# A fused forward and backward pass: loading a third weight slab ahead of the rows, fixed places for the turns, and a PSUM half for the convolution

## The chip, the cores and the metric

The kernel runs on one core of a Trainium2 chip. A core has TensorE (PE), which multiplies matrices and also transposes; VectorE (DVE); ScalarE (ACT); GpSimd (POOL) and SyncE (SP). Every engine works off its own list of instructions in order. SP, ACT and POOL also issue DMAs, and such an issue stands in the engine's order like any other instruction. The metric is the device time of one execution in microseconds (us), as the median of several runs.

## What is computed

Cut to what matters, with S = 2048 rows, D = 1024 columns and F = 3584 hidden columns in bf16:

```python
x  = A_q
xn = layernorm(x)                                   # per row
# A: gated long convolution
k_shift = sum over 4 taps of shifted k * A_shift_k  # along the rows
kv = k_shift * v
y  = irfft(rfft(kv) * rfft(A_ssm_k))[:S] + kv * A_ssm_D   # per column
s  = xn * y
# B: bilinear unit
g, u = xn @ w_gate, xn @ w_up
bm = (g * u) @ w_down
out = x + s * silu(bm)
# returned: out and the gradients of all ten inputs for a given grad_out
```

## The kernel before

Rows are handled in blocks of 128 (16 blocks), columns of D in 8 groups of 128 (`dc`), and the hidden columns F in 14 slabs of 256 (`SLW`); a slab is 256 columns of both `w_up` and `w_gate` (1 MB). The kernel first forms g and u for all blocks and slabs ("units"), with the forward convolution laid between the units; then the down product, the output, and the backward pass, which is by far the larger part of the time.

**The start stage.** Row blocks come in six chunks, `chunks = [(0,1), (1,1), (2,2), (4,4), (8,4), (12,4)]` (first block, number of blocks). For each chunk `ln_load` (line 555) issues the load of the rows on SP, and `layer_norm` (line 566) does the statistics on DVE (`bn_stats`, lines 572 to 577), a square root on ACT (`half_r`, line 580), the rest of the factor and the normalisation on DVE (line 591), and a store of the normalised rows to DRAM (`XNd`) on POOL. The normalised rows are turned by PE (transposes into the PSUM tile `tr`; lines 597, 608 and 617) and copied by ACT into the transposed rows `XNT` (tiles U0 to U3; lines 598, 609 and 618). The turns of chunks 8 and 12 are not made at once: `turn_late` makes them after the first block of the next unit.

**A unit.** `gu_unit(sl, b0, n, w, tick)` multiplies n blocks from b0 by slab sl. For each block, 8 matmuls (line 656, one for each `dc`, 128x512) fill one of two PSUM buffers `psg`; ACT casts the buffer into `gut` (line 658). After the unit's last block, ACT issues the store of `gut` to `GUd` (`sta`, line 72). During the next unit, DVE multiplies the two halves (`hN`, line 213), POOL stores that to `Hd` (line 66), and some blocks later PE transposes `hN` (line 689), ACT copies it (`hT`, lines 691 and 693) and SP stores it to `HTd`.

**The order of loads.** SP issues the loads of chunks 0 and 1, slab 0, chunk 2, slab 1, and then chunks 4, 8 and 12. A slab is two DMAs of 512 KB:

```python
for a, wsrc in ((0, B_w_up), (1, B_w_gate)):
    last = eng.dma_start(out=w[:, :, a, :], in_=wsrc[:, fs].rearrange("(dc p) f -> p dc f", p=P))
```

The units of the start stage are, by chunk:

```python
([(0, 0)], [(1, 0), (0, 1), (1, 1)], [(2, 0), (2, 1)], [(3, 0), (3, 1)], [(4, 0)], [(5, 0)])[i]
```

where the first number is the chunk's place in `chunks` and the second the slab. After the start stage come slab 1 for chunks 8 and 12, and then slabs 2 to 13 for all blocks. Every DMA signals its end on one of a few semaphores that are used in turn; a DMA whose turn falls on a semaphore still in use waits on its issuing engine for the earlier one to end.

**The convolution.** `conv_forward` is a generator of small pieces: loads of k and v on POOL, the four shifted products of k on DVE (`shift`), and the transforms, which are matmuls against a table `TF` on PE (PSUM tiles `psF` and, for the inverse, `psY`) with products on DVE between them. The table is made by ACT from angles that DVE masks (line 174). A `tick` after each block of a unit pumps as many pieces as the share of work done so far asks for, so the pieces' places among the units are fixed when the program is built. The down product (`bm_first`, `late_mm`; matmul at line 994) then goes on pumping, and the inverse pieces of the convolution stand at steps `at = (52, 55, 58, 61)` of it.

Of the kernel before, what the change touches and what calls it, by code (L numbers as in the profile page):

```python
# [19 lines left out]
def build_kernel(  # L20
# [11 lines left out]
    nc = tc.nc  # L32
# [254 lines left out]

    def fwd8_half(x, i, SP, psp, first=None, held=False):

        pe_us[0] += 0.87  # L290
        for j in range(2):
# [4 lines left out]
            nc.scalar.copy(out=SP[:, :, j], in_=ps[:].rearrange("p s k x -> p s (k x)"))  # L296

    def fwd8(SPs, X, W, C, ahead, late=False):
# [225 lines left out]
    ps_tr = pool("ps_tr", 1, space=PSUM)  # L524
    ps_gu = pool("ps_gu", 2, space=PSUM)
    ps_st = pool("ps_st", 4, space=PSUM)
# [19 lines left out]

    def load_slab(sl, eng):
        w = fw.tile([P, DC, 2, SLW], BF16, name="wslab")
# [12 lines left out]

    tr_ln, act_copy = [None], [None]
    turn_rows = []

    def layer_norm(b0, n, x4):
# [22 lines left out]
        for i in range(n):  # L588
            b = b0 + i
            q, qi = divmod(b, 4)  # L590
            last = V.tensor_scalar(x4[:, i, :], x4[:, i, :], mv[:, i, 0:1], RSTD[:, b:b + 1], op0=SUB, op1=MUL)
            if b < 2:
                for hh in range(2):
                    ps = ps_st.tile([P, 4, P], BF16, name="tr")
                    for dc in range(4):
                        d0 = (4 * hh + dc) * P
                        tr_ln[0] = nc.tensor.transpose(ps[:, dc, :], x4[:, i, d0:d0 + P], ident[:])
                    act_copy[0] = nc.scalar.copy(out=XNT[0][:, 4 * hh:4 * hh + 4, b * P:b * P + P], in_=ps[:])
                if b == 0:
                    with tc.issue_after(tr_ln[0].ins):  # L600
                        keep_busy(10)
                continue
            if b0 >= 8:
                turn_rows.append((x4[:, i, :], q, qi))
                continue
            ps = ps_st.tile([P, DC, P], BF16, name="tr")
            for dc in range(DC):
                tr_ln[0] = nc.tensor.transpose(ps[:, dc, :], x4[:, i, dc * P:(dc + 1) * P], ident[:])
            act_copy[0] = nc.scalar.copy(out=XNT[q][:, :, qi * P:(qi + 1) * P], in_=ps[:])
# [30 lines left out]
    def gu_unit(sl, b0, n, w, tick):  # L640

        if n == 4:
            turn_of[0] += 1
            if turn_of[0] % 3 == 0 and sl < NSL - 2:
                gut = U[5][:, 2048:4096].rearrange("p (a i f) -> p a i f", a=2, i=4)
            else:
                gut = fg.tile([P, 2, 4, SLW], BF16, name="gut")
            hN = fg.tile([P, 2, 4, P], BF16, name="hN", bufs=3)
        else:
            gut = lnp.tile([P, 2, 2, SLW], BF16, name="gut_s", bufs=6)  # L650
            hN = lnp.tile([P, 2, 2, P], BF16, name="hN_s", bufs=6)
        for i in range(n):
            q, qi = divmod(b0 + i, 4)
            ps = ps_gu.tile([P, 512], F32, name="psg")
            for dc in range(DC):
                gu_mm[0] = nc.tensor.matmul(ps[:], XNT[q][:, dc, qi * P:(qi + 1) * P],  # L656
                                            w[:, dc].rearrange("p a f -> p (a f)"), start=(dc == 0), stop=(dc == DC - 1))
            nc.scalar.copy(out=gut[:, :, i], in_=ps[:].rearrange("p (a f) -> p a f", a=2))  # L658
# [42 lines left out]

    conv_state = {"forward": True, "filters": True}

    y_first = [None]

    def conv_forward():
# [83 lines left out]
        def half(ds, x, i, first=None):  # L790
            if (ds, int(first is not None)) not in EIGHT:
                return fwd4_half(x, i, cf, ps_cv, first)
            SP = cf.tile([P, 2, 2, 512], F32, name="SP", bufs=2)
            fwd8_half(x, i, SP, ps_cv, first, True)
            return SP

        def transform(ds, kind, sp, X, C, ahead, step):

            if ds == 7 and kind == 1:
                S_["forward"] = False  # L800
            if (ds, kind) in EIGHT:
                W = fwd4_buf(cs)[:].rearrange("p a b c x -> p (a b c) x")
                for n, w in enumerate(fwd8(sp, X, W, C, ahead, True)):
                    if n in (0, 2, 4, 6):
                        step()
                    yield net(w)
                return
# [24 lines left out]
        for ds in range(8):  # L832
# [16 lines left out]
            next(tl, None)  # L849
            room = cf.tile([P, 4, 256], F32, name="room", tag="hx")[:] if eight else None  # L850
            yield from transform(ds, int(ds > 0), sph, HX if ds else KX, room, nop1 if eight else lambda c: h_rows(ds + 1, c),
# [7 lines left out]
            if eight:  # L859
                h_rows(ds + 1, 1)  # L860
            if ds == 7:
                cf.release()
                S_["filters"] = False
            st(HFd[ds], HX[:])
# [14 lines left out]
        for _ in tl:  # L879
# [9 lines left out]
    chunks = [(0, 1), (1, 1), (2, 2), (4, 4), (8, 4), (12, 4)]  # L889
    xs = [(b0, n, u8((4, 6, 7)[b0 // 4 - 1], a=4) if n == 4 else lnp.tile([P, n, D], BF16, name=f"x{b0}")[:])  # L890
          for (b0, n) in chunks]
    for c in xs[0:2]:
# [3 lines left out]
    slabs.append(load_slab(1, nc.sync)[0])  # L896
    for c in xs[3:]:
        ln_load(*c)

# [38 lines left out]
    ps_st.release()  # L938
    ps_cv = pool("ps_cv", 2, space=PSUM)
# [57 lines left out]

    def bm_first(fcs):
        for fc in fcs:
            for i in range(2):  # L1000
                mm = bm_mm(pss[i], lambda fc: HT0[fc // 16][:, fc % 16], i, fc)
            if fc % 2 == 1:
                tick()
        return mm

    assert not conv_state["forward"]
    ps_cv.release()
    ps_bm = pool("ps_bm", 2, side="right", space=PSUM)
    pss = [ps_bm.tile([P, D], F32, name="psbm") for i in range(2)]
    with tc.issue_after(bm_first(range(4)).ins):  # L1010
        flush()
    for p_ in (ps_gu, fg, fw):
        p_.release()
# [19 lines left out]
    mh = [pool("mh0", 1, side="right")]  # L1033
    ps_bx = pool("ps_bx", 1, space=PSUM)

# [291 lines left out]
    def late_mm(n):  # L1327
        b, fc = divmod(n, NF)
        b += 2
        if fc == 0:  # L1330
            if 2 < b < 5 and done < 0:
                bms.append(out_of(ps_of[b - 1], room[1][:, b - 3]))
            ps_of[b] = (ps_bx if b % 3 == 2 else ps_bm).tile([P, D], F32, name="psbm")
        with tc.issue_after(inv_mm[0].ins) if b < 5 else nullcontext():
# [39 lines left out]
    for bp in range(2, 8):  # L1374
# [18 lines left out]
        for i in range(2):  # L1393
# [7 lines left out]
            gate(2 * bp + i, ps_of[2 * bp + i])  # L1401
    for p_ in (ps_bx, ps_tr, ps_y, ps_bm, mi, mo, mt, mh[1], mh[0]):
        p_.release()
# [363 lines left out]
```

## Time and profile before

| | before |
|---|---|
| median of three runs | 1917.38 us (1917.29 to 1918.71) |
| the profiled execution's own time | 1918.36 us |
| its span in the profile | 1916.6 us |
| TensorE's granted clock | 1.0 |
| PE busy | 1905.7 us, 99% |
| DVE busy | 1557.1 us, 81% |
| ACT busy | 640.0 us, 33% |
| POOL busy | 334.5 us, 17% |
| DVE busy from 100 to 400 us | 99.2, 99.0 and 99.1 of each 100 us |
| DMA engines' busy share from 10 to 20 us | 1.09 |

The span runs from the first to the last instruction in the trace; the time of the execution holds 1.76 us more around it. Lines such as L656 are line numbers of the kernel before. In the timeline a line gives the start, the busy time, the engine, the source line, the operation, its output and inputs, and in brackets how long the engine stood idle ahead of it and what released it.

### The profile page before, as it was taken

To read this page: it belongs to the slowest core of one execution; us is meant where nothing else is said; L and a number is where in the kernel's file an instruction comes from. 1 tells how busy PE (TensorE), PEld (TensorE's weight loads), DVE (VectorE), ACT (ScalarE), POOL (GpSimd) and SP (SyncE) were. 2 spreads that over 40 slices of the span, in tenths; PEclk is the share of its full clock that TensorE was granted. 3 is DMA by queue.
4 is the path that set the end of the run, shared out by engine and by line. 5 is a ranking of instruction groups with operands and counts; after the bars stand their busy time and mean duration, and the time that the engine had idled before them with its cause. 6 is when DMAs were issued, how large, how long until landed. Compare 5 with 4: busy or idle time off the path is not lost. (4 is left out here: it accounts for less than half of the span.)

```text
span 1916.6 us, 27330 instructions
## 1 busy us (share of the span) xinstructions
PE 1905.7 (99%) x10915; PEld 1024.9 (53%) x10915; DVE 1557.1 (81%) x1723; ACT 640.0 (33%) x946; POOL 334.5 (17%) x465
## 2 busy tenths in 40 slices
PE   8999999999999999999999999999999999999999
PEld 5555555545544456666666665664444444444444
DVE  8999999999997556887999999999995205788862
ACT  5864555646433233432222222222222102011121
POOL 5121212111113220001031221111212101111120
PEclk9999999999999999999999999999999999999999
DMA  8776867668679997677887698585787999999962
GB/s 293 271 261 216 265 209 234 211 234 299 237 246 287 316 287 250 205 240 236 269 271 261 220 263 270 180 286 177 217 255 173 206 205 191 184 184 195 193 180 97
DMA packets 425487, 444.28 MB, mean 232 GB/s; under 512 B 268784, under 2 KB 343180, under 8 KB 410896
## 3 DMA queue, kind: packets, MB, share of 16 engines
q1 hardware_dynamic: 367888, 239.03, 46.9%
q0 software_dynamic: 41152, 174.15, 29.1%
q10 hardware_dynamic: 16320, 29.36, 4.1%
q8 instruction: 85, 1.39, 0.3%
q14 instruction: 42, 0.34, 0.1%
HBM read 193.87 MB, written 189.84 MB: 200 GB/s over the span
## 5 line engine op out<-in xcount | busy, mean ns | idle before, releaser
L656 PE MATMUL psg<-wslab,U 128*128 128x512 bf16 x1792 | 407.3, 379 | 3.0 <-DMA wslab<-in_B_w_gate_dram 2.0
L1458 PE MATMUL psb<-U,U 128*128 128x512 bf16 x1792 | 397.1, 379 | 0.0
L1603 PE MATMUL psx<-U,dgut 128*128 128x512 bf16 x1536 | 333.0, 379 | 0.5 <-DVE dxn L213 0.5
L1603 PEld LDWEIGHTS <-dgut 128*128 128x128 bf16 x1792 | 175.3, 98 | 212.1 <-issue 0.8
L1458 PEld LDWEIGHTS <-U 128*128 128x128 bf16 x1792 | 175.2, 98 | 198.0
L656 PEld LDWEIGHTS <-U 128*128 128x128 bf16 x1792 | 172.2, 98 | 187.4 <-issue 2.5
L1441 PE MATMUL psb<-wdt,U 128*128 128x256 bf16 x1792 | 205.6, 273 | 0.0
L213 DVE TENSOR_TENSOR W<-W 128x1024 f32<-128x1024 f32 (+1 forms) x192 | 189.1, 1001 | 4.2
L1441 PEld LDWEIGHTS <-U 128*128 128x128 bf16 x1792 | 175.3, 98 | 29.2
L1541 PE MATMUL psb<-U,U 128*128 128x512 bf16 x816 | 177.3, 379 | 0.0
L1463 ACT CAST wb<-psb 128x512 bf16<-128x512 f32 x112 | 65.6, 586 | 315.4 <-PE psb L1458 310.5
L1208 DVE SCALAR_TENSOR_TENSOR dkp<-dkT,kT 128x1024 bf16<-128x1024 bf16 (+2 forms) x64 | 78.3, 1224 | 104.0 <-DMA dkT<-DKSHd 102.2
L994 PE MATMUL psbm<-U,ht 128*128 128x512 bf16 x672 | 146.0, 379 | 0.0
L1541 PEld LDWEIGHTS <-U 128*128 128x128 bf16 x896 | 87.4, 98 | 104.3
L658 ACT CAST gut<-psg 128x512 bf16<-128x512 f32 x156 | 91.3, 588 | 120.0 <-PE psg L656 119.1
L1635 ACT ACTIVATE dx_t<-dxn 128x1024 bf16<-128x1024 f32 x15 | 15.9, 1057 | 324.2 <-DVE dxn L213 320.3
L994 PEld LDWEIGHTS <-ht 128*128 128x128 bf16 x672 | 65.6, 98 | 78.0
L213 DVE TENSOR_TENSOR U<-U,dht 128x2048 bf16<-128x2048 bf16 x56 | 68.3, 1221 | 46.4 <-ACT dht L1443 46.4
L1443 ACT CAST dht<-psb 128x512 bf16<-128x512 f32 x112 | 65.6, 587 | 116.3 <-PE psb L1441 116.3
L66 POOL DMA_DIRECT2D Hd<-hN x54 | 37.1, 686 | 292.3 <-DVE hN L213 289.4
L1582 ACT CAST wbs<-psb 128x512 bf16<-128x512 f32 x51 | 29.9, 586 | 145.4 <-PE psb L1541 137.3
L213 DVE TENSOR_TENSOR W<-SP 128x1024 f32<-128x1024 f32 x64 | 74.5, 1219 | 2.5 <-ACT SP L296 1.7
(261 smaller groups left out, 2386.3 us busy)
## 6 DMA issues: line engine op xcount, KB each, us to landing
U<-GUd SPq DMA_DIRECT2D x28, 1024.0 KB, 8.7
DGd<-U SPq DMA_DIRECT2D x28, 1024.0 KB, 6.5
GUd<-gut ACTq DMA_DIRECT2D x39, 512.0 KB, 5.5
out_dram<-wb SPq DMA_DIRECT2D x112, 128.0 KB, 4.8
U<-Hd SPq DMA_DIRECT2D x14, 1024.0 KB, 5.9
Hd<-hN POOLq DMA_DIRECT2D x54, 256.0 KB, 4.2
HTd<-hT SPq DMA_DIRECT2D x52, 256.0 KB, 3.9
ht<-HTd SPq DMA_DIRECT2D x18, 512.0 KB, 7.7
```

Of the source, the lines that this page charges most:

```text
L66: ins = nc.gpsimd.dma_start(out=out, in_=in_)
L213: pinned(V.tensor_tensor(o, a, b, op))
L656: gu_mm[0] = nc.tensor.matmul(ps[:], XNT[q][:, dc, qi * P:(qi + 1) * P], w[:, dc].rearrange("p a f -> p (a f)"), start=(dc == 0), stop=(dc ...
L658: nc.scalar.copy(out=gut[:, :, i], in_=ps[:].rearrange("p (a f) -> p a f", a=2))
L994: mm = nc.tensor.matmul(ps[:, dh * 512:(dh + 1) * 512], ht(fc)[:, i * P:(i + 1) * P], WD[fc // 4][:, fc % 4, dh * 512:(dh + 1) * 512], sta ...
L1208: ins = V.scalar_tensor_tensor(prod[:].rearrange("p r d -> p (r d)")[:, lo:H], dkT[:, 0, lo:H], 1.0, kT[:, 0, 13 + m + lo:13 + m + H], op0 ...
L1441: nc.tensor.matmul(ps[:, x * SLW:(x + 1) * SLW], DBMT[2 * hf + g][:, dc, (b % 4) * P:(b % 4 + 1) * P], wdt[:, dc, :], start=(dc == 0), sto ...
L1443: nc.scalar.copy(out=dht[:, 2 * e:2 * e + 2].rearrange("p b f -> p (b f)"), in_=ps[:])
L1458: nc.tensor.matmul(ps[:], XN[b // 4][:, b % 4, dc * P:(dc + 1) * P], dgus[b // 8][:, :, b % 8], start=(b == 0), stop=(b == NB - 1))
L1463: nc.scalar.copy(out=wb[:, dc % 2].rearrange("p a f -> p (a f)"), in_=ps[:])
L1541: nc.tensor.matmul(ps, h[:, f, b, :], DBM[b // 4][:, b % 4, dh * 512:(dh + 1) * 512], start=(b == 0), stop=(b == NB - 1))
L1603: nc.tensor.matmul(ps[:, dh * 512:(dh + 1) * 512], t[n][:, f, i * P:(i + 1) * P], WGU[n][:, f, dh * 512:(dh + 1) * 512], start=(n == 0 and ...
```

## The change

Four things are edited in the start stage. Slabs 0, 1 and 2 are each loaded as four DMAs (up and gate, each in two halves of `dc`), and slab 2 is loaded into a tile of its own (U7) directly after slab 1, ahead of the rows of chunk 4; chunk 4's rows come as two DMAs, and chunk 12's rows are loaded later, into a tile `x_own` that first holds blocks 0 to 3. The units of slab 2 for blocks 0 to 3 run in the start stage. The turns of blocks 1, 2 and 3 are put ahead of fixed units (`turn_next`), those of blocks 4 to 15 after fixed blocks (`TURN_AT`). After the start stage, slab 2 goes over blocks 4 to 15, and slabs 3 to 11 follow as before.

Further on, the two `psF` banks become tagged tiles of one pool that the down product also uses: `bm_first` starts with one bank while the convolution may keep the other, forward pieces can be split in two (`cv_parts`), the pumping starts at other counts, and the inverse pieces stand at steps `at = (64, 67, 70, 73)`.

```diff
     def load_slab(sl, eng, w=None):
+        if w is None:
+            w = fw.tile([P, DC, 2, SLW], BF16, name="wslab")
         fs = slice(sl * SLW, (sl + 1) * SLW)
-        for a, wsrc in ((0, B_w_up), (1, B_w_gate)):
-            last = eng.dma_start(out=w[:, :, a, :], in_=wsrc[:, fs].rearrange("(dc p) f -> p dc f", p=P))
+        n = DC // 2 if sl < 3 else DC
+        for d0 in range(0, DC, n):
+            for a, wsrc in ((0, B_w_up), (1, B_w_gate)):
+                last = eng.dma_start(out=w[:, d0:d0 + n, a, :],
+                                     in_=wsrc[d0 * P:(d0 + n) * P, fs].rearrange("(dc p) f -> p dc f", p=P))
...
+        elif b0 == 4:
+            for r in (0, 2):
+                ld(x4[:, r:r + 2, :], xq[:, c, r0 + r:r0 + r + 2, :])
...
                 if b == 0:
+                    turn_first()
                     with tc.issue_after(tr_ln[0].ins):
                         keep_busy(10)
+                else:
+                    turn_next.append(((1, 0), turn_first))
                 continue
-            if b0 >= 8:
+            if b0 >= 4:
                 turn_rows.append((x4[:, i, :], q, qi))
                 continue
...
+            turn_next.append(((0, 2), turn_second))
...
+    TURN_AT = ((1, 2, 1), (0, 4, 2), (0, 8, 1))
...
-            hN = lnp.tile([P, 2, 2, P], BF16, name="hN_s", bufs=6)
+            hN = lnp.tile([P, 2, 2, P], BF16, name="hN_s", bufs=8)
...
-            if i == 0:
+            if (sl, b0, i) in TURN_AT:
                 turn_late()
...
+    class Banks:
+        n, alone = 0, False
+
+        def tile(self, shape, dt, name):
+            self.n = 0 if self.alone else 1 - self.n
+            return ps_cv.tile(shape, dt, name=name, tag=f"psF{self.n}")
...
-                return fwd4_half(x, i, cf, ps_cv, first)
+                return fwd4_half(x, i, cf, cv_banks, first)
             SP = cf.tile([P, 2, 2, 512], F32, name="SP", bufs=2)
-            fwd8_half(x, i, SP, ps_cv, first, True)
+            fwd8_half(x, i, SP, cv_banks, first, True, cv_parts if cv_banks.alone else None)
...
     slabs.append(load_slab(1, nc.sync)[0])
-    for c in xs[3:]:
-        ln_load(*c)
+    slabs.append(load_slab(2, nc.sync, u8(7, "p (c a f) -> p c a f", c=DC, a=2))[0])
+    ln_load(*xs[3])
+    ln_load(*xs[4])
...
+        if i == 2:
+            ln_load(*xs[5])
...
-        for i_, sl in ([(0, 0)], [(1, 0), (0, 1), (1, 1)], [(2, 0), (2, 1)], [(3, 0), (3, 1)], [(4, 0)], [(5, 0)])[i]:
+        for i_, sl in ([(0, 0)], [(1, 0), (0, 1), (1, 1), (0, 2), (1, 2)], [(2, 0), (2, 1), (2, 2)], [(3, 0), (3, 1)],
+                       [(4, 0)], [(5, 0)])[i]:
+            while turn_next and turn_next[0][0] == (i_, sl):
+                with tc.issue_after(gu_mm[0].ins):
+                    turn_next.pop(0)[1]()
             gu_unit(sl, *xs[i_][0:2], slabs[sl], nop)
...
-    cnt = [-5]
+    cnt = [-4]
...
-        if cnt[0] == -4:
-            pump((SHIFT_W + 4.05) / F_TOTAL)
...
-    pump((SHIFT_W + 3.95) / F_TOTAL)
+    pump((SHIFT_W + 4.05) / F_TOTAL)
     for i_ in (4, 5):
         gu_unit(1, *xs[i_][0:2], slabs[1], tick)
-    for sl in range(2, NSL - 2):
+    for b0 in (4, 8, 12):
+        gu_unit(2, b0, 4, slabs[2], tick)
+    for sl in range(3, NSL - 2):
...
+    cv_banks.alone = True
+    bm_bank = lambda n: ps_cv.tile([P, D], F32, name="psbm", tag=f"psF{n}")
+    pss.append(bm_bank(1))
+    bm_first(range(4), (0,))
+    ps_gu.release()
+    ps_bm = pool("ps_bm", 1, side="right", space=PSUM)
+    pss.append(ps_bm.tile([P, D], F32, name="psbm"))
+    with tc.issue_after(bm_first(range(4), (1,)).ins):
         flush()
...
-    at = (52, 55, 58, 61)
+    at = (64, 67, 70, 73)
```

More of the change, by code (lines that the diff above doesn't have):

```diff
@@ L286, in stt, with fwd8_half, part @@
             tc.keep_in_program_order(ins)
-    def fwd8_half(x, i, SP, psp, first=None, held=False):
+    def fwd8_half(x, i, SP, psp, first=None, held=False, parts=None):
         pe_us[0] += 0.87
-        for j in range(2):
+        def part(j):
             r = 2 * i + j
@@ L296, in fwd8_half @@
             nc.scalar.copy(out=SP[:, :, j], in_=ps[:].rearrange("p s k x -> p s (k x)"))
+        for j in range(2):
+            if parts is None:
+                part(j)
+            else:
+                parts.append(lambda j=j: part(j))
     def fwd8(SPs, X, W, C, ahead, late=False):
@@ L524, in build_kernel @@
     ps_tr = pool("ps_tr", 1, space=PSUM)
-    ps_gu = pool("ps_gu", 2, space=PSUM)
+    ps_gu = pool("ps_gu", 2, side="right", space=PSUM)
     ps_st = pool("ps_st", 4, space=PSUM)
@@ L563, in build_kernel @@
     turn_rows = []
+    turn_next = []
     def layer_norm(b0, n, x4):
@@ L592, in layer_norm, with turn_first, turn_second @@
             if b < 2:
[L593 to L598, printed above, removed]
+                def turn_first(b=b):
+                    for hh in range(2):
+                        ps = ps_st.tile([P, 4, P], BF16, name="tr")
+                        for dc in range(4):
+                            d0 = (4 * hh + dc) * P
+                            tr_ln[0] = nc.tensor.transpose(ps[:, dc, :], x4[:, 0, d0:d0 + P], ident[:])
+                        act_copy[0] = nc.scalar.copy(out=XNT[0][:, 4 * hh:4 * hh + 4, b * P:b * P + P], in_=ps[:])
                 if b == 0:
+                    turn_first()
                     with tc.issue_after(tr_ln[0].ins):
                         keep_busy(10)
+                else:
+                    turn_next.append(((1, 0), turn_first))
                 continue
-            if b0 >= 8:
+            if b0 >= 4:
                 turn_rows.append((x4[:, i, :], q, qi))
                 continue
[L606 to L609, printed above, removed]
+            def turn_second(i=i, q=q, qi=qi):
+                ps = ps_st.tile([P, DC, P], BF16, name="tr")
+                for dc in range(DC):
+                    tr_ln[0] = nc.tensor.transpose(ps[:, dc, :], x4[:, i, dc * P:(dc + 1) * P], ident[:])
+                act_copy[0] = nc.scalar.copy(out=XNT[q][:, :, qi * P:(qi + 1) * P], in_=ps[:])
+            turn_next.append(((0, 2), turn_second))
         c, r0 = divmod(b0, 8)
         return last, root, st(xnn[:, c, r0:r0 + n, :], x4[:, 0:n, :])
+    TURN_AT = ((1, 2, 1), (0, 4, 2), (0, 8, 1))
     def turn_late():
@@ L700, in build_kernel @@
     SHIFT_W = 8 * 2.3
-    conv_state = {"forward": True, "filters": True}
+    conv_state = {"filters": True}
+    class Banks:
[3 more added lines that the diff above has]
+            return ps_cv.tile(shape, dt, name=name, tag=f"psF{self.n}")
+    cv_banks = Banks()
+    cv_parts = []
     y_first = [None]
@@ L791, in half @@
             if (ds, int(first is not None)) not in EIGHT:
-                return fwd4_half(x, i, cf, ps_cv, first)
+                return fwd4_half(x, i, cf, cv_banks, first)
             SP = cf.tile([P, 2, 2, 512], F32, name="SP", bufs=2)
-            fwd8_half(x, i, SP, ps_cv, first, True)
+            fwd8_half(x, i, SP, cv_banks, first, True, cv_parts if cv_banks.alone else None)
             return SP
         def transform(ds, kind, sp, X, C, ahead, step):
-            if ds == 7 and kind == 1:
-                S_["forward"] = False
+            while cv_parts:
+                cv_parts.pop(0)()
             if (ds, kind) in EIGHT:
@@ L803, in transform @@
                 for n, w in enumerate(fwd8(sp, X, W, C, ahead, True)):
+                    if (ds, kind, n) == (7, 1, 2):
+                        cf.release()
+                        S_["filters"] = False
                     if n in (0, 2, 4, 6):
@@ L849, in conv_forward @@
             next(tl, None)
-            room = cf.tile([P, 4, 256], F32, name="room", tag="hx")[:] if eight else None
+            room = None
+            if eight:
+                room = krow[:].rearrange("p a b d -> p (a b d)")[:, NB * P:2 * NB * P].bitcast(F32).rearrange("p (a x) -> p a x", a=4)
             yield from transform(ds, int(ds > 0), sph, HX if ds else KX, room, nop1 if eight else lambda c: h_rows(ds + 1, c),
@@ L860, in conv_forward @@
                 h_rows(ds + 1, 1)
-            if ds == 7:
-                cf.release()
-                S_["filters"] = False
             st(HFd[ds], HX[:])
@@ L889, in build_kernel @@
     chunks = [(0, 1), (1, 1), (2, 2), (4, 4), (8, 4), (12, 4)]
-    xs = [(b0, n, u8((4, 6, 7)[b0 // 4 - 1], a=4) if n == 4 else lnp.tile([P, n, D], BF16, name=f"x{b0}")[:])
-          for (b0, n) in chunks]
+    x_own = lnp.tile([P, 4, D], BF16, name="x_own")
+    xs = [(b0, n, u8((4, 6)[b0 // 4 - 1], a=4) if b0 in (4, 8) else x_own[:, b0 % 4:b0 % 4 + n, :]) for (b0, n) in chunks]
     for c in xs[0:2]:
@@ L938, in build_kernel @@
     ps_st.release()
-    ps_cv = pool("ps_cv", 2, space=PSUM)
+    ps_cv = pool("ps_cv", 1, space=PSUM)
     pump, drain, step = make_pump(conv, F_TOTAL)
-    cnt = [-5]
+    cnt = [-4]
     NT = 24 * 8.0 + 33
@@ L996, in bm_mm, with bm_first @@
         return mm
-    def bm_first(fcs):
+    pss = []
+    def bm_first(fcs, blocks=(0, 1)):
         for fc in fcs:
-            for i in range(2):
+            for i in blocks:
                 mm = bm_mm(pss[i], lambda fc: HT0[fc // 16][:, fc % 16], i, fc)
-            if fc % 2 == 1:
-                tick()
-        return mm
[L1006 to L1010, printed above, removed]
+            if fc % 2 == 1 or len(blocks) == 1:
+                if cv_parts:
+                    cv_parts.pop(0)()
+                if fc % 4 == 3 or len(blocks) == 2:
+                    tick()
+        return mm
+    cv_banks.alone = True
[6 more added lines that the diff above has]
+    with tc.issue_after(bm_first(range(4), (1,)).ins):
         flush()
-    for p_ in (ps_gu, fg, fw):
+    for p_ in (fg, fw):
         p_.release()
@@ L1033, in build_kernel @@
     mh = [pool("mh0", 1, side="right")]
-    ps_bx = pool("ps_bx", 1, space=PSUM)
+    assert not cv_parts
     ddo = const.tile([P, 8], BF16, name="ddo")
@@ L1332, in late_mm @@
                 bms.append(out_of(ps_of[b - 1], room[1][:, b - 3]))
-            ps_of[b] = (ps_bx if b % 3 == 2 else ps_bm).tile([P, D], F32, name="psbm")
-        with tc.issue_after(inv_mm[0].ins) if b < 5 else nullcontext():
+            ps_of[b] = ps_bm.tile([P, D], F32, name="psbm") if b % 3 == 1 else bm_bank(b % 3 // 2 ^ 1)
+        with tc.issue_after(inv_mm[0].ins) if n < at[3] + 4 or b < 5 else nullcontext():
             return bm_mm(ps_of[b], hts[b // 2][0], b % 2, fc)
-    at = (52, 55, 58, 61)
+    at = (64, 67, 70, 73)
     for n in range(at[3] + 1):
@@ L1401, in build_kernel @@
             gate(2 * bp + i, ps_of[2 * bp + i])
-    for p_ in (ps_bx, ps_tr, ps_y, ps_bm, mi, mo, mt, mh[1], mh[0]):
+    for p_ in (ps_cv, ps_tr, ps_y, ps_bm, mi, mo, mt, mh[1], mh[0]):
         p_.release()
```

3 lines of the change are left out of this document (1 added, 2 removed).

## The prediction

> **What bounds the kernel now.** I read the busy times, then the waits of TensorE, then the first 70 us as a timeline by engine.
>
> ```profile
> PE 1905.7 (99%) x10915; PEld 1024.9 (53%) x10915; DVE 1557.1 (81%) x1723; ACT 640.0 (33%) x946; POOL 334.5 (17%) x465
> ```
>
> TensorE (PE) is busy 1905.7 of 1916.6 us at full granted clock. The built programs of before and after hold the same matmuls and transposes and the same VectorE (DVE) work, so only PE's idle time can change. Its waits:
>
> ```profile
> PE psg L656 <- DMA wslab<-in_B_w_gate_dram: 2.0, 2, 1.0
> ...
> PE tr L608 <- DVE U L591: 0.9, 1, 0.9
> PE psg L656 <- ACT gut L658: 0.8, 2, 0.6
> PE tr L617 <- DVE U L591: 0.7, 1, 0.7
> ...
> PE psg L656 <- ACT U L598: 0.2, 1, 0.2
> ```
>
> All of these but a bit of the third lie between 8 and 41 us, where the change works; PE's timeline places them (start, us, then in brackets the idle before):
>
> ```profile
> 9.26 1.67 PE L656 MATMUL psg<-wslab,U 128*128 128x512 bf16 x7 [0.99 <-DMA wslab<-in_B_w_gate_dram]
> ...
> 11.83 1.90 PE L656 MATMUL psg<-wslab,U 128*128 128x512 bf16 x8 [0.24 <-ACT U L598]
> 14.71 2.10 PE L656 MATMUL psg<-wslab,U 128*128 128x512 bf16 x9 [0.97 <-DMA wslab<-in_B_w_gate_dram]
> ...
> 25.67 1.99 PE L608 MATMUL tr<-ident,U 128*128 128x128 bf16 x32 [0.95 <-DVE U L591]
> ...
> 35.03 1.99 PE L617 MATMUL tr<-ident,U 128*128 128x128 bf16 x32 [0.72 <-DVE U L591]
> ...
> 39.99 3.61 PE L656 MATMUL psg<-wslab,U 128*128 128x512 bf16 x16 [0.59 <-ACT gut L658]
> ```
>
> The brackets sum to 4.46 us. Sixteen matmuls in 3.61 us start 0.216 us apart while the page gives each 0.379, so a gap shown is 0.163 short: six gaps are **5.44 us**. That is all this change can remove there.
>
> **Part 1: the start.** Three edits act together: slab 2 is loaded right behind slab 1 and its units for blocks 0 to 3 run early; slabs 0 to 2 come in four pieces; the turns of rows get fixed places.
>
> *What goes.* Two more units (16 matmuls, 3.5 us, for blocks 0 and 1) and a third for blocks 2 and 3 stand ahead of block 4's turns, so the rows of blocks 4, 8 and 12 are normalised before their turns come: the 0.95 and 0.72 (1.11 and 0.89 with the correction) vanish, and so does the 0.59 (0.75). The slab waits shrink, because half a slab is enough to begin.
>
> *What comes: first unit.* The first copy into XNT, ahead of unit (0,0), costs 0.41 (its block's normalisation ends at 9.89 + 0.55) and 0.56 (the copy), and the second half of slab 0 0.25: 1.22 us.
>
> *What comes: a store on ACT.* In the built order the store of unit (0,0)'s `gut` (line 72) stands on ACT ahead of the second half of block 1's copy into XNT. It waits for its semaphore's previous user, and with eight more load pieces that is now the last gate piece of slab 1; in before it was a piece of slab 0. In before slab 1's packets ended at 13.94 and PE saw them at 14.71. A store on ACT does hold back the copy behind it:
>
> ```profile
> 16.63 0.59 ACT L658 CAST gut_s<-psg 128x512 bf16<-128x512 f32 x1 [2.17 <-PE psg L656]
> 17.25 0.52 ACTq L72 DMA_DIRECT2D GUd<-gut_s  x1
> 17.81 1.93 ACT L609 COPY U<-tr 128x1024 bf16<-128x1024 bf16 x2 [0.59 <-PE tr L608]
> ```
>
> So in after the store issues at about 14.65, the copy ends at 14.65 + 0.55 + 0.54 = 15.8, and the fifth matmul of unit (1,0), which PE reaches at about 12.4, waits 3.4 us. [...]
>
> *What comes: a square root on ACT.* Block 4's rows now queue behind 1 MB more. Slabs took 4.8 and 5.0 us for 1 MB, block 4's rows 3.6 (13.06 to 16.67): 13.94 + 4.4 for slab 2 + 1.4 for half of block 4 + 0.75 until its user sees it = 20.5. The statistics up to `vpe` took 5.69 us (18.28 to 23.97); three `hN` products now stand among them (0.3 each): 27.1. On ACT `half_r` waits for that, and behind it stands the `gut` copy of unit (1,2): 27.1 + 0.3 + 0.6 = 28.0. PE wants that PSUM buffer at 15.8 + 44 matmuls x 0.216 + 18 transposes x 0.057 (a turn's 32 took 1.83) = 26.3: it waits, with its notice, 1.8 us (1.6 to 2.6, since a product took 1.10 us beside POOL's copies at 17.25 where a pair took 0.49).
>
> Sum to 28 us: 1.22 + 3.4 + 1.8 = **6.4** (to 7.2) against 5.44.
>
> *What comes: k rows.* The second new place is near 65 us.
>
> ```profile
> 36.64 0.54 POOL L66 DMA_DIRECT2D XNd<-U  x1 [1.57 <-DVE U L591]
> 37.17 3.33 POOL L66 DMA_DIRECT2D k<-in_A_k_dram  x4
> ```
>
> POOL issues the loads of k behind the store of block 8's rows. These are normalised 6.2 us later in after (42.6 for 36.4), because on DVE two `hN` products of slab 2 now stand before their last steps and wait for PE. In before the last of k was there at about 50.9, when the shift's first product began:
>
> ```profile
> 51.00 2.29 DVE L213 TENSOR_TENSOR U<-k,Wbc 128x4096 bf16<-128x4096 bf16 x1 [0.91 <-PE tr L617]
> ```
>
> In the built order that product now stands on DVE ahead of the mask steps (0.69 each) that the first `TF` on ACT (1.15) needs, and behind that `TF` on ACT queue a `gut` copy, `hT` (1.0), four copies into XNT (3.76) and the next `gut`. With k there at 55.0 this chain ends at 65.9, and PE, which has some 37 us of work after 28.0, wants its buffer at 64.9: 1.0 us idle, and each us later for k adds one. Shifted by 6.2, k comes at 57.1 (3.1 idle); if its transfers, 9.5 to 11.4 us in before beside two 1 MB POOL transfers, are quicker, at 55. I take 56: **2.0 us** (1.0 to 3.2).
>
> *Hidden.* Six more issues on SP by 0.43 to 1.35 us (its slab rows) lie under transfers already queued. Block 12's load into the shared row buffer waits for the stores of blocks 0 to 3 on POOL; its rows are normalised after block 8's, more than 15 us later. If late it would delay the turns at about 56 us one for one.
>
> *Pieces.* Slab 0's packets end at 8.48, slab 1's begin at 8.94: a seam of 0.46, my upper price for a piece; none shows between the two pieces inside a slab, so I take zero. [...]
>
> **Part 2: convolution and PSUM.** Conv pieces come 5 to 6 us of PE work later. DVE, which feeds them, was busy over 99 of each 100 us from 100 to 400; its chain starts about 8.5 us later, PE's pieces 5.6 + 3.0. The slack in the trace (PE start less the end of DVE's product) is 4.1 us at 74, 2.3 at 185, 1.4 at 298, 3.5 at 421, so nothing waits: zero, and 1.4 is what DVE may lose before each further us costs one. In the built order the last forward conv matmul still comes ahead of the first down matmul (line 994), so nothing runs on into the down product; only the inverse's pieces come nine steps of down matmuls later, where their product already had 2.4 us of slack. Zero; if the cover were gone, the amount by which the inverse is late.
>
> **Sum.** 6.4 + 2.0 - 5.44 = +3.0. Span 1916.6 + 3.0 = 1919.6, the profiled execution 1918.36 + 3.0 = 1921.4. The median of before is 0.98 below its profiled execution, so **1920.4 us**. About 0.2% (3.8 us: below 1913.5, above 1921.2) is what a measurement of this kernel can tell from no change.
>
> **Rivals.**
> - *The change works (faster).* ACT's two waits don't bite: slab 1's last piece lands with 1 MB before 12.4, and block 4's rows early. For: the saturated stretch can be ordered differently by queues. Against: slab 1 ended at 13.94 with the same bytes ahead. Idle 1.2 + 0 to 1.0 - 5.44: 1913.1 to 1914.2. Chance 0.13, half of it past the bound.
> - *Nothing in sum.* Both waits half as long: 1.2 + 2.6 + 1.0 - 5.44 = -0.6; with part 2 inert in the built order, the change doesn't do what it says. 1916.7 to 1918. Chance 0.12.
> - *k late (slower).* K rows land at 58 or later, because the store ahead of them or v's rows share the engines: idle 4 at 65 us, or 5 at 59, and the first part at its 7.2. 1917.38 + 7.2 + 4 - 5.44 = 1923.1. It passes the bound from k at 56.0 with 7.2, from 56.8 with 6.4. For: the plain shift gives 57.1. Chance 0.25.
> - *Seams (slower).* Each of the four extra pieces up to slab 1 costs 0.46: slab 1 lands 1.84 later, and so does the store on ACT: 1922.2. The trace shows no seam inside a slab. [...] Chance 0.08.
>
> The forecast keeps 0.42, its own range 1919.1 to 1922.3 (6.2 with 1.0 to 7.2 with 3.2).
>
> **Chances.** Faster: 0.07. Slower: k late 0.24, seams 0.07, the forecast's upper end 0.12: 0.43. Same: the rest, 0.50. Range 1916.0 to 1924.0: it leaves out most of the first rival (0.12) and 0.08 above.
>
> **What would show it.** In PE's timeline of after: a gap of about 3 us near 12.4 after four of eight matmuls, released by ACT; one near 26 released by a `gut` copy; none before the turns of blocks 4, 8, 12; one of 1 to 3 near 65. On ACT, the first store at 14 to 15. First shift product at 55 to 57. A first gap under 1 us, or a new PE wait on DVE after 100 us, proves me wrong.

## The result, and the profile after

| | before | after |
|---|---|---|
| median of the runs | 1918.71 us (9 runs, 1917.29 to 1922.15) | 1923.42 us (9 runs, 1921.26 to 1924.82) |
| span of the profiled execution | 1916.6 us | 1920.6 us |
| ratio to before | | 1.0023, 95% interval 1.0013 to 1.0033 |

The change makes the kernel slower by 0.23%, some 4.4 us. Its runs were taken beside nine of the kernel before, whose median, 1918.71, lies above that of the first three (1917.38); the ratio is the surer figure. The profile after opens like the one before:

```profile
PE 1906.8 (99%) x10915; PEld 1023.4 (53%) x10915; DVE 1556.2 (81%) x1725; ACT 639.1 (33%) x948; POOL 335.0 (17%) x467
```

```profile
PE psg L679 <- ACT U L613: 3.6, 2, 2.8
PE psg L679 <- DMA wslab<-in_B_w_gate_dram: 1.7, 2, 1.0
...
PE psF L235 <- ACT SP L257: 1.1, 2, 0.8
PE psg L679 <- ACT U L681: 0.8, 1, 0.8
...
PE psF L235 <- DVE kv L213: 0.2, 1, 0.2
```

In PE's waits (source lines of the new kernel; L679 is the unit's matmul, L613 the copy into XNT) the two waits on normalised rows before the turns of blocks 4 and 8 are gone, and so is all but 0.2 of the wait on `gut`; a wait on ACT's copy into XNT of 2.8 us has come, and waits of the convolution. PE's timeline shows where:

```profile
9.69 1.02 PE L679 MATMUL psg<-wslab,U 128*128 128x512 bf16 x4 [1.04 <-DMA wslab<-in_B_w_gate_dram]
...
11.88 1.04 PE L679 MATMUL psg<-wslab,U 128*128 128x512 bf16 x4 [0.72 <-ACT U L613]
13.63 0.38 PE L679 MATMUL psg<-wslab,U 128*128 128x512 bf16 x1 [0.71 <-DMA wslab<-in_B_w_gate_dram]
16.84 6.69 PE L679 MATMUL psg<-wslab,U 128*128 128x512 bf16 x19 [2.83 <-ACT U L613]
```

From 12.8 to 16.84 PE runs a single matmul. The last line holds the surprise: 19 matmuls took 6.69 us, where 16 took 3.61 before. The busy time by stretches names the reason (the third column from the end is the granted clock, the share of full speed at which PE was clocked):

```profile
12.00:16.00 4.00, 1.29 (x5) 0.29 (x3) 2.35 (x7) 0.00 (x0) 0.00 (x0) 0.87 1.16 328
16.00:22.00 6.00, 5.16 (x13) 1.90 (x14) 3.44 (x10) 1.52 (x4) 2.99 (x4) 0.52 1.09 367
```

At half the clock, the matmuls started 0.427 us apart and not 0.217; twelve of them cost 2.4 us. The 0.87 of the first line shows that the clock fell before 16 us, while PE still stood idle; stretches cut finer put the half clock from 14.94 to 21.76. ACT's timeline shows the gap's origin, the store that waits and the copy behind it:

```profile
15.58 0.58 ACTq L72 DMA_DIRECT2D GUd<-gut_s  x1
16.20 0.58 ACT L613 COPY U<-tr 128x512 bf16<-128x512 bf16 x1 [4.38 <-DMA wslab<-in_B_w_gate_dram]
```

To see where the 4.4 us arise I take, at a given time, the time less the work that PE has done by then (0.2165, 0.1095 or 0.0565 us for a matmul of 512, 256 or 128 columns). After minus before, this lag is 2.35 us at 60 us, 3.06 at 72, 2.95 at 130, 4.23 at 350 and 4.44 at 1600. So the start costs 2.35, the gap at 66 us 0.7, the convolution 1.4. Of the start, the first 8 us gave 0.48 back, for in this profile PE's first transposes started 0.056 us apart from 4.7 us on (0.107 until then) and in that of before from 6.5; from 8 to 60 us 2.83 are lost, near the 2.9 that the gaps of 1.20, 0.88, 0.88 and 2.99 and the half clock's 2.4 make less the 5.44 of before. At the end the lag's difference is 3.74, for the one profiled execution of before had a single gap of 0.71 at 1610 us that the other had not.

### The profile page after: what moved, and what is told of

Read it like the earlier page. It is cut to its first block, busy times and chain, and to the rows that moved or that the text cites. A ratio compares the mean times of both kernels' runs of the same rounds, so it can differ in the third digit from the quotient of the medians.

```text
span 1920.6 us, 27355 instructions
## 1 busy us (share of the span) xinstructions
PE 1906.8 (99%) x10915; PEld 1023.4 (53%) x10915; DVE 1556.2 (81%) x1725; ACT 639.1 (33%) x948; POOL 335.0 (17%) x467
## 4 chain that ended last, share of the span: by engine, by line
PE 86%; DVE 10%; issue 2%; ACT 1%; DMA 1%; SPq 0%; POOL 0%; ACTq 0%; DVEq 0%
PE psb L1508 20%; PE psx L1653 20%; PE psg L679 10%; PE psb L1491 10%; PE psbm L1036 10%; PE psb L1591 9%; DVE W L213 3%; DVE KX L213 2%; DVE HX L213 2%; PE psF L235 2%; DVE U L213 1%; DVE m L213 1%; PE psY L452 1%; DVE hN L213 1%; PE psY L1202 1%
## 5 line engine op out<-in xcount | busy, mean ns | idle before, releaser
L679 PE MATMUL psg<-wslab,U 128*128 128x512 bf16 x1664 | 380.2, 381 | 6.3 <-ACT U L613 3.6
L679 PEld LDWEIGHTS <-U 128*128 128x128 bf16 x1792 | 172.9, 98 | 194.9 <-issue 7.1
```

## The experiments

Each kernel is the changed one with the edit shown, unless said otherwise. Ratios are to the kernel before, run beside it, with 95% intervals. Gaps are from one matmul's start to the next less the matmul's own time.

**The store behind the copy.**

```diff
-        sta(GUd[sl, b0 // 8][...], gut[:, :, 0:n])          # unit (0, 0) only
...
+                with tc.issue_after(act_copy[0].ins):       # after block 1's copies
+                    first_sta.pop()()
```

> The changed kernel with one edit: the store of unit (0,0)'s gut is issued on ACT behind block 1's second copy into XNT instead of ahead of it. Theory A (the store's wait for the last gate piece of slab 1 holds the copy, and the half clock from 16.8 to 21.6 us follows from that gap): the gap of 2.99 us ahead of 16.84 goes, matmuls stay 0.217 us apart, the turns of blocks 2 and 3 begin near 19 us instead of 23.4; but the gut copy of unit (1,2) still stands behind block 4's square root (about 27.4), so the second block of unit (2,0) begins near 28.2 instead of 29.55 after about 3 us idle: the time falls by about 1.3 us only, or not at all if that second gap halves the clock as the first did. Rival B (PE waits for slab 1's data in any case): a wait of 2 us or more on the slab's gate piece takes the place of the wait on the copy, and the turns begin later than 21 us.

Measured: 1923.1 us, ratio 1.0026 (1.0016 to 1.0036). The first gap is gone and the turns of blocks 2 and 3 begin at 17.53 instead of 23.37. PE's and ACT's timelines then show the next one:

```profile
27.81 2.54 PE L680 MATMUL psg<-wslab,U 128*128 128x512 bf16 x8 [3.79 <-ACT gut_s L682]
```

```profile
27.08 0.20 ACT L595 ACTIVATE half_r<-vpe 128x4 f32<-128x4 bf16 x1 [5.57 <-DVE vpe L592]
27.19 0.57 ACT L682 CAST gut_s<-psg 128x512 bf16<-128x512 f32 x1
```

The square root of block 4 holds the `gut` copy, PE waits 3.95 us, and from 28.9 to 32.3 its matmuls are again 0.43 apart (granted clock 0.72 in the mean from 28 to 34 us). By 45 us all 5.8 us are given back: the lag there is 11.5 with this edit and 11.6 without. Rival B falls: the wait on slab 1 in its place was 0.28 us.

**Transposes in the gap.** They are matmuls of the identity with itself, whose result is not used.

```diff
+                if (sl, b0, dc) == (0, 1, 3):
+                    spare = ps_st.tile([P, 4, P], F32, name="tr")
+                    for e in range(50): nc.tensor.matmul(spare[:, e % 4, :], ident[:], ident[:], ...)
```

> The changed kernel with 50 transposes of the identity into a spare PSUM tile put on PE behind the fourth matmul of unit (1,0); they compute nothing that is used and take 50 x 0.056 = 2.8 us of a gap that is there anyway. Theory A (the half clock is the answer to PE's gap): the fifth matmul still starts near 16.8, but the matmuls behind it are 0.217 us apart and not 0.427, so PE reaches the turns of blocks 2 and 3 about 2.4 us earlier (near 21); then block 4's square root holds the gut copy of unit (1,2) to 28.5, and of the 2.4 us about 1.0 is left in the time. Rival C (the half clock comes from something else at that time, such as the DMA load or the state after the warm-up): the matmuls from 16.8 to 21.6 stay 0.427 apart and the time does not change.

Measured: 1924.21 us, ratio 1.0034 (1.0021 to 1.0047). The matmuls behind the gap ran at full clock, 1.00 from 12 to 22 us:

```profile
15.96 4.49 PE L679 MATMUL psg<-wslab,U 128*128 128x512 bf16 x20 [0.52 <-ACT U L613]
...
28.45 2.32 PE L679 MATMUL psg<-wslab,U 128*128 128x512 bf16 x8 [3.66 <-ACT gut_s L686]
```

So rival C falls: with PE at work in the gap no half clock came. The time did not fall as I expected, since in this build the square root had moved one place further ahead on ACT and stood before the `gut` copy of unit (0,2): a second gap of 3.8 us, with a half clock of its own (0.72 in the mean from 28 to 34 us). As a price this run is not clean.

**The root later, without and with the transposes.**

```diff
-            root = nc.scalar.activation(half_r, vpe, ACT.Sqrt, scale=0.25)
+            with tc.issue_after(gut_copy[0].ins):   # blocks 4 to 7: after unit (2, 0)
+                root = nc.scalar.activation(half_r, vpe, ACT.Sqrt, scale=0.25)
...
```

What follows the root for these blocks, the normalisation, the store of the rows and the spreading of the shift's taps, is put into the program behind unit (2,0) with it.

> The changed kernel with one edit: the square root of blocks 4 to 7 stands on ACT behind the gut copies of unit (2,0) instead of ahead of that of unit (1,2). Theory A: the gap of 2.99 us and the half clock are untouched, and in the changed kernel PE reached that point so late that this order costs nothing: the time is the same within 0.5 us. Rival D (the square root already costs PE time there, as the prediction had it): 1 us or more faster.

Measured: 1921.53 us, ratio 1.0023 (1.0014 to 1.0032), the same as the changed kernel. The square root costs nothing as long as the first gap makes PE late.

> The changed kernel with the square root of blocks 4 to 7 behind the gut copies of unit (2,0) and 50 transposes of the identity, whose result is not used, behind the fourth matmul of unit (1,0): the same order on ACT as with the root later alone, the same wait for the copy, but PE busy in the gap. Theory A (the half clock answers PE's gap, and is a cost of its own of about 2.4 us): the fifth matmul starts as late as with the root later alone (near 16), all matmuls behind it are 0.217 us apart, no second gap follows, and the time falls by 2 to 2.5 us against the root later alone (ratio to the kernel before about 1.0010 for 1.0023). Rival C (what the half clock costs is taken up by later waits): the matmuls are 0.217 apart but the time stays within 0.7 us of the root later alone.

Measured: 1919.34 us, ratio 1.0012 (1.0003 to 1.0021), beside 1.0023 for the root later alone. Of these two kernels, the lines of the copy's wait and the busy time from 16 to 22 us, first without the transposes:

```profile
15.77 7.09 PE L689 MATMUL psg<-wslab,U 128*128 128x512 bf16 x19 [3.19 <-ACT U L621]
...
16.00:22.00 6.00, 6.00 (x16) 2.11 (x15) 2.54 (x9) 1.17 (x2) 4.06 (x5) 0.54 1.09 388
```

and with them:

```profile
16.74 4.49 PE L689 MATMUL psg<-wslab,U 128*128 128x512 bf16 x20 [1.28 <-ACT U L621]
...
16.00:22.00 6.00, 5.26 (x37) 2.91 (x38) 3.01 (x9) 2.59 (x6) 3.09 (x4) 1.00 1.10 370
```

The copy's wait ends no earlier (in this profile a microsecond later), but 20 matmuls take 4.49 us where 19 took 7.09, and the whole kernel is 2.2 us shorter by the medians (1921.53 and 1919.34). Here the half clock is priced apart from the wait, by work that computes nothing; the two ratios' intervals overlap from 1.0014 to 1.0021, so the price is known to a microsecond or so.

**Both moved.** The store behind the copy and the root later.

> The changed kernel with both edits: the first store behind block 1's second copy, and the square root of blocks 4 to 7 behind the gut copies of unit (2,0). Theory A (the store's wait, its half clock, and the square root behind them are one chain): no gap over 1 us from 13 us on, full clock, the turns of block 4 near 30.5 instead of 35.1, and the time 3 to 5 us shorter, near that of the kernel before. Rival B (slab 1's and block 4's data set the start): less than 2 us.

Measured: 1917.47 us, ratio 0.9998 (0.9990 to 1.0007), against 1.0023 for the changed kernel. No gap over 0.62 us before 130 us, full clock, the turns of block 4 at 29.30 instead of 35.07:

```profile
16.00:22.00 6.00, 5.95 (x40) 3.11 (x40) 2.83 (x8) 3.59 (x5) 4.66 (x5) 1.00 1.08 391
```

```profile
29.30 1.95 PE L651 MATMUL tr<-ident,U 128*128 128x128 bf16 x32
```

The two orders on ACT and the clock that follows from them cost as much as the whole loss, 4.8 us by the ratios; each alone returns none of it. The waits of the convolution are still there (0.36, 0.95, 0.33 and 0.52); what the change saves in the start pays for them, and no more.

**Slabs in two DMAs.** `n = DC` in `load_slab`.

> The changed kernel with slabs 0 to 2 in two DMAs each, as in the kernel before; nothing else. With fewer DMAs the first store on ACT falls to the semaphore of block 2's rows, long landed. Theory A: no wait of ACT ahead of block 1's second copy; the first unit starts near 9.2 (whole slab 0) and unit (0,1) near 14.7 (whole slab 1), the turns of blocks 2 and 3 begin near 18.2 instead of 23.4; then PE waits for the gut copy of unit (1,2) behind block 4's square root until about 28.4, a gap of about 4 us, and if a gap of that size halves the clock for 5 us, 2.4 us are lost there: in sum the time changes by -1 to +1.5 us. Rival S (pieces cost a fixed time each, so four pieces land slabs later): slab 1 is complete about 1 us or more earlier than in the changed kernel, where its last piece was seen at 15.58.

Measured: 1921.48 us, ratio 1.0021 (1.0010 to 1.0032). The store no longer waits, and PE goes on at once when slab 1 is there, then stops at the root:

```profile
14.54 4.48 PE L679 MATMUL psg<-wslab,U 128*128 128x512 bf16 x20 [1.38 <-DMA wslab<-in_B_w_gate_dram]
...
27.62 1.89 PE L679 MATMUL psg<-wslab,U 128*128 128x512 bf16 x8 [2.42 <-ACT gut_s L681]
```

This second gap is 2.58 us and not the 4 I expected, and 8 matmuls behind it take 1.89 us: full clock, 1.00 from 22 to 34 us. Rival S is not borne out. In two pieces slab 1 is seen at 14.54 and in the changed kernel's profile at 15.58, a microsecond later, as S asks; but with four pieces it is seen at 14.4 with the store moved, at 14.51 with the root later and at 15.48 with root and transposes: the spread is not the pieces'.

**The kernel before with slabs 0 and 1 in four DMAs.**

> The kernel before with slabs 0 and 1 in four DMAs each; nothing else of the change. The first store on ACT falls to the semaphore of block 2's rows. Theory A: unit (0,0) starts near 7.7 instead of 9.26 and PE is ahead by 0.5 to 1 us until the turns of block 4, which wait for normalised rows at 25.7 as before: the time is the same within 0.5 us. Rival S (pieces cost a fixed time each): slab 1's last piece and the rows of blocks 4 to 15 land 1 us or more later, and the time rises by that.

Measured: 1919.19 us, ratio 1.0006 (0.9997 to 1.0014). Unit (0,0) starts at 8.05 instead of 9.26, PE is 0.55 us ahead at the turns of blocks 2 and 3 (16.09 for 16.65), and block 4's turns start at 25.61 (25.67 before): the lead is spent on waiting for the rows. The pieces alone neither help nor harm by more than the interval.

**Rows of block 4 ahead of slab 2.**

```diff
+    ln_load(*xs[3])
     slabs.append(load_slab(2, nc.sync, ...)[0])
-    ln_load(*xs[3])
```

> The changed kernel with the load of rows 4 to 7 issued ahead of slab 2 instead of behind it. The first store's semaphore is the same. Theory A: the gap of 2.99 us and the half clock stay; rows 4 to 7 are normalised about 3 us earlier, and the first pieces of slab 2 land about 3.5 us later, near 22, still ahead of 24.3 where PE wants them: the time is the same within 1 us. Rival B (order of loads is what the change gets wrong): 2 us or more faster.

Measured: 1923.42 us, ratio 1.0028 (1.0017 to 1.0039). Block 4's statistics begin at 18.32 instead of 20.57, the gap (3.27 us) and the half clock (0.72 in the mean from 16 to 22 us) stay. Theory A's result, and rival B falls.

**k rows early.**

```diff
+        if i == 3:
+            with tc.issue_after(xsts[3].ins):
+                next(conv)          # the loads of k, ahead of block 8's store
...
-                for _ in range(2):
-                    next(conv)
+                next(conv)
```

> The changed kernel with the loads of k issued on POOL ahead of the store of block 8's rows. Theory A (late rows of k make DVE's shift late; that costs the gap of 0.96 us at 66 us and the small waits of the convolution between 190 and 330 us): k is there before the mask steps end, the shift begins near 56.2 instead of 56.92, the gap at 66 us falls to about 0.2, the waits from 100 to 350 us, 2.9 in sum, shrink by less than 0.7: 1 to 1.5 us faster. Rival E (what is late is DVE's chain as a whole, not k): at most 0.8 us at 66 us and nothing later.

Measured: 1924.17 us, ratio 1.0034 (1.0022 to 1.0046). Both theories missed. DVE's timeline shows one of the shift's products put ahead of block 12's normalisation, and another still ahead of the mask:

```profile
49.71 2.29 DVE L213 TENSOR_TENSOR KX<-k,Wbc 128x4096 bf16<-128x4096 bf16 x1 [1.43 <-DMA k<-in_A_k_dram]
...
56.30 2.29 DVE L213 TENSOR_TENSOR U<-k,Wbc 128x4096 bf16<-128x4096 bf16 x1
...
59.10 0.69 DVE L174 TENSOR_SCALAR m<-m 128x1024 int32<-128x1024 int32 x1
```

The mask was 0.6 us earlier than in the changed kernel (59.73), while PE was 1.8 us earlier (its half clock lasted 3.4 us in this profile and not 6.8), and the gap near 65 us grew from 0.96 to 1.98. The waits of the convolution stayed as they were (0.36, 0.96, 0.32, 0.49 for 0.35, 0.95, 0.33, 0.51): late k does not make them.

**The later pieces one block later.**

```diff
-  (cnt[0] + 6.5)
+  (cnt[0] + 6.5 if cnt[0] <= 1 else max(7.5, cnt[0] + 5.5))
```

> The changed kernel with the convolution's pieces after the first transform placed one block of matmuls (1.73 us of PE work) later among the units; the first pieces (up to 90 us) and all else stay. In the changed kernel the first pieces stand 6.9 to 7.8 us of PE work later than in the kernel before and all later ones only 5.65 later, while DVE, which stands idle for 4.9 us until the first of them, is busy without a break from then on. Theory F (the waits of PE between 190 and 390 us, 0.35, 0.95, 0.33, 0.51 and 0.28, come from this shift of the later pieces against the first): all but 0.2 of each goes, the waits over 0.25 us from 100 to 450 us fall from 2.4 to under 0.5 us and the time by about 1.5 us. Rival G (they come from the late rows of k or from the order of ACT's copies): they stay.

Measured: 1922.56 us, ratio 1.0024 (1.0015 to 1.0033). All five named waits are gone, so their cause is the place of the later pieces against the first, as theory F has it. But three others came, of 0.35, 0.45 and 0.39 us, that PE's waits put down to ACT:

```profile
PE psY L463 <- ACT yf L806: 0.7, 3, 0.3
```

The waits over 0.25 us from 100 to 450 us fell from 2.4 to 1.2 and not to 0.5, and the time shows nothing of it; a gain of 1.2 us is less than the ratio's interval can show. Theory F was right on the cause and wrong on what is won.

**Four edits and five.** Store, root, k ahead, and all products of the shift behind the mask; then the later pieces one block later too.

> The changed kernel with the first store behind block 1's second copy, the square root of blocks 4 to 7 behind the gut copies of unit (2,0), the loads of k ahead of the store of block 8's rows, and DVE's mask steps ahead of all products of the shift. Theory F: the shift begins near 52 us instead of 57.8 (store and root alone), DVE then stands idle for 3 us or more until the first pieces, and the waits between 190 and 390 us are the same as without the early k: the time is that of the kernel with store and root alone (ratio 1.000 to the kernel before) within 0.7 us. Rival G (late k makes the convolution's waits): 1 us or more shorter than that.

Measured: 1916.83 us, ratio 0.9995 (0.9986 to 1.0003). The waits at 188, 201, 205 and 315 us are 0.34, 0.96, 0.33 and 0.52, those of the changed kernel, and DVE stands idle before the first pieces:

```profile
DVE W L215 <- ACT SP L299: 4.4, 1, 4.4
```

Theory F's result; rival G falls.

> The kernel with the four edits (store, root, k, mask) and with the later pieces of the convolution one block later as well. Theories A and F together: idle of about 3 us up to 16 us, no half clock, no gap near 60 to 66 us, no wait over 0.3 us between 190 and 390 us; against the kernel before, 5.4 us of idle become 3 in the start and 3.9 stay about 3 after it: 2 to 3 us faster than the kernel before (ratio about 0.9987), unless the single waits near 480 and 1610 us, which differ from run to run by up to 2 us, hide it.

Measured: 1917.24 us, ratio 0.9998 (0.9989 to 1.0006). Its profiled execution has the shortest span of all, 1914.5 us, but the timed runs, from 1916.28 to 1920.5, do not bear that out. Single waits of PE differ from profile to profile: near 480 us, before a `gut` buffer whose store has not landed, from none to 2.06 us, and near 1610 us from none to 2.34. No kernel here is shown to beat the one before; the four edits come nearest.

## Why the prediction was right or wrong

The direction and the size were right: +3.0 us forecast, some 4.4 measured, 1923.42 within 1916.0 to 1924.0, but past the forecast's own range (1919.1 to 1922.3) and past the 1921.2 at which I set "slower". Counted by the ratio from the 1917.38 that the forecast started from it would be 1921.8, inside the forecast's range and still past "slower". The chance of slower was 0.43, that of the same 0.50. The terms:

- **What goes (5.44):** right. No wait on rows stands before the turns of blocks 4, 8 and 12, and 0.59 on `gut` is gone. Of the units that I put ahead of block 4's turns, the third, slab 2 for blocks 2 and 3, stands behind them: from 11.88 to 35.07 PE runs 72 unit matmuls and not 88. The sum did not use it.
- **First unit (1.22):** about right in kind, low in size: gaps of 0.33, 1.20 and 0.88, 2.4 us. The half slab I priced at 0.25 cost 1.20, and the copy of block 1 another 0.88.
- **The store on ACT (3.4):** shown. In the profile before ACT waits for no DMA in the first 80 us; in the changed kernel ACT stands idle for 4.38 us ahead of the copy, and the profile puts that down to the gate piece of the slab. The gaps are 0.88 and 2.99 us with one matmul between, 3.9 in sum. The store's wait ended at 15.58 instead of 14.65, PE came some 0.35 later than I had it, and the matmul between the gaps, on slab 1, I had not placed; the three make the difference. Of the 15.58, up to a microsecond is chance: in the other profiles with four pieces and the store in its place the wait ended between 14.51 and 15.48.
- **The half clock (not in the sum):** this is the step that failed. I priced the gap at its length; it cost 2.4 us more, about 2 when measured alone. The profile before could not show it, with no gap over 1.2 us after its first matmul and a granted clock of 1.0. PE was not wholly idle ahead of the fall either: from 11.88 to 14.94 it ran five matmuls, 1.08 us of work. I had foreseen the gap and left this out.
- **The root on ACT (1.8):** in the changed kernel nothing, because PE came later than 26.3: its second block of unit (2,0) started at 29.55 and found the copy done at 28.5. Behind the first gap stands this one: with the store moved it was 3.95 us.
- **k rows (2.0):** k's product began at 56.92, where I took 56 and the plain shift gave 57.1; the gap was 0.96. That it was not 2.9 has the same reason: PE came there 1.5 us later than I had it, at 66.4. Two lines of DVE's timeline, the second for the next point:

```profile
56.92 2.29 DVE L213 TENSOR_TENSOR U<-k,Wbc 128x4096 bf16<-128x4096 bf16 x1 [0.73 <-DMA k<-in_A_k_dram]
...
83.14 4.63 DVE L213 TENSOR_TENSOR W<-SP 128x1024 f32<-128x1024 f32 x4 [4.89 <-ACT SP L297]
```

- **Convolution (0):** wrong, 1.3 us between 130 and 350 us. The second line above is why. I compared the start of DVE's chain with PE's pieces; but DVE waits 4.89 us for the first piece, and its unbroken work is counted from there. PE's first pieces stand 6.5 to 7.8 us of PE work later than before and most later ones 5.65, so the slack shrank by one to two microseconds: the start of the pieces, not k, was the anchor. I also looked at slack for `kv` alone, not at the copies of `SP`, whose wait (0.95) was the largest. Moving the pieces removed these waits and brought smaller ones. By the sign that I had set, a new wait of PE on DVE after 100 us, this part was wrong: one of 0.2 us on `kv` came, beside the larger ones on ACT.
- **Part 2, the PSUM half:** zero, as forecast, from 600 us on (the lag's difference, 4.45 at 600 and 4.44 at 1600, does not move). It was not undone by itself.

Of the rivals, the faster one had its two waits as conditions; moving both on ACT gave the 4.8 us back and ended level with the kernel before (0.9998), not 3 to 4 us ahead. "Nothing in sum" fell with the ratio's lower end of 1.0013. "k late" had the right sign and the wrong place. "Seams" fell: the pieces cost nothing that shows (1.0006 for the kernel before in four). Slab 1 was seen at 14.54 in two pieces and between 14.4 and 15.58 in four.

## What to carry to other kernels

Price a wait of the bound engine by its length and by what it does to the clock behind it (here some 2 us more for a gap of 2.99), and ask which wait stands next in line: here two waits on ACT hid each other, and undoing either alone gave nothing. When a change adds transfers, look again at which earlier transfer each later issue waits for; that assignment alone held a store on ACT, and the copy behind it, for 4.4 us; in two pieces the same store did not wait. And if another engine works without a break, count its slack from the point where it last waited, not from where its work begins.

## What the runs showed of the hardware

- A half clock came with gaps of 2.99 us (changed kernel), 3.27 (rows of block 4 ahead), 3.35 (root later), 3.82 (transposes, second gap) and 3.95 (store moved), and with one of about 2.5 (k rows early). It did not come with one of 2.58 (slabs in two DMAs; clock 1.00 from 22 to 34 us). Why the two near 2.5 us differ is not shown.
- In the changed kernel a single matmul, at 13.63, stood ahead of the gap of 2.99 us, 0.88 behind the one before it, and the half clock came all the same. With 50 matmuls of the identity put in there the clock stayed at 1.00 from 12 to 22 us, in both kernels that had them.
- In the changed kernel the granted clock fell at 14.94, 1.9 us before PE's next matmul at 16.84, and was back at 1.00 at 21.76, 6.8 us later. The mean clock of longer stretches gives 6.8 us at half for the root later (0.84 from 12 to 16 us, 0.54 from 16 to 22), and 3.4 with the store moved and with the transposes (0.72 from 28 to 34 in each), with the rows of block 4 ahead (0.72 from 16 to 22) and with the k rows early (0.94 from 12 to 16, 0.76 from 16 to 22).
- Four loads of k issued on POOL within 3.3 us took 8.5 to 10.0 us to land in the changed kernel and 14.0 to 15.4 with store and root moved. There a broadcast of 1 MB had been issued 2.1 us ahead of them, in the changed kernel 6.2 us ahead; a store of 1 MB went just ahead of them in both. That the broadcast is the cause is not shown. Issued 4.5 us earlier, they landed no earlier: the first product began at 57.83 for 56.92.
